# Second product of the last four tiles of the first block: from float32 to three float32r passes

## The chip, the cores and the metric

One core of one Trainium2 chip runs the kernel. The metric is the device time of one execution in microseconds (us); of several executions the median is taken. TensorE (PE) does the matrix products, VectorE (DVE) and ScalarE (ACT) the elementwise work, and SyncE (SP) issues the transfers.

## The reference

Two feed-forward layers follow a linear attention. Only the first layer's second product (`g @ w_out` of `_moe_ref`) is touched by the change.

```python
def _attn_ref(q, k, v, g_norm):
    kv = np.einsum('bhsd,bhse->bhde', k, v)
    out = np.einsum('bhsd,bhde->bhse', q, kv)
    rms = np.sqrt(np.mean(out * out, axis=-1, keepdims=True) + 1e-06)
    return (out / rms * g_norm).astype(np.float32)

def _moe_ref(x, w_in, w_out, a, b):        # 4608 tokens, 512 -> 2048 -> 512
    h = x @ w_in
    P = a[0] + a[1] * h + a[2] * h**2 + a[3] * h**3
    Q = 1.0 + np.abs(b[0]) * np.abs(h) + np.abs(b[1]) * h**2
    return ((P / (Q + 1e-06)) @ w_out).astype(np.float32)

def _moe2_ref(x, w_in, w_out):             # again 512 -> 2048 -> 512
    h = x @ w_in
    g = np.where(h >= 1, h, np.where(h <= -1, 0.0, (h + 1) ** 2 / 4))
    return (g @ w_out).astype(np.float32)
```

The attention's output, laid out as 4608 x 512, is the x of the first layer, whose output is the x of the second.

## The kernel before

**Stages.** Nine blocks of 512 tokens (`T`, `NB`) go through the first layer (phase 0, `ffn_step(0, j, f, s)`, block j), each in 16 tiles f of 128 hidden features (`NF`). After them block 0 goes through the second layer in the same manner (phase 1), and then the other eight blocks in pairs by a seven-product scheme (`ffn2_in`, `ffn2_out`), which uses combinations of weights and of activations that earlier stages prepare (`prepare`, `prepare_out`, `x_combinations`).

**A product in float32r.** A float32 value is split into a high part (a copy to float32r, made by ACT) and a low part (the difference, made by DVE). A product is then three matmuls: high by high, high by low, low by high. The first product of a tile is 4 such triples (lines 670 to 672) into the accumulator `h`, of which there are two (ring `h`): the first product of a tile cannot start before the tile two places earlier has been read out of its `h`, which DVE does last with the cubic's `t` (line 213, `t<-t,na,h`). The second product is 4 triples (lines 719 to 721) into `acc0` to `acc3`.

**The first block is different.** Its second products are made in float32 (`native`, line 717): 4 matmuls to a tile, which the chip runs as two records each, so 8 records to a tile. They need neither a split of `g` nor a split of the weights: DVE writes `gh` at once, and the decoded weight `w32[f]` (ring `wol`) is used as it is. The weights come packed and are decoded by `decode` (two ACT and two DVE instructions) while the first block runs. The high part of an output weight (ring `woh`) is made with the decoding; its low part by `weight_low`, with the key `NF + f + 0.5`, which places it one block later (line 312); the second block's second products need it.

**What sets the order.** Every instruction is recorded with a cost and a key. `Program.order` plays the list through: on each engine, whenever it comes free, the ready instruction with the lowest key is next. Tiles live in rings: the n-th tile of a ring of b buffers, counted by keys, waits for every reader of tile n - b. So a key or a count that changes in one ring can move instructions on all engines from there on.

**Rings that matter.** `wol` has 17 buffers (`NF + 1`): it holds five pieces of v at the very start, ten more of other batches, then the 16 decoded output weights and their 16 low parts, and later the 16 low parts of the second layer's output weights, which `prepare_out` makes (line 390) and also stores to DRAM for the last stage (`wod`). `dec` has 2 buffers, for weights being decoded. All transfers of these stages are issued by SP, in order.

Of the kernel before, what the change touches and what calls it, by code (L numbers as in the profile page):

```python
# [12 lines left out]
I32 = mybir.dt.int32  # L13
# [30 lines left out]
class Program:  # L44
# [16 lines left out]
    def op(self, engine, cost, key, fn, reads=(), writes=(), slack=0.0):  # L61
        i = len(self.ops)
        deps = set()
        for t in reads:
            if t.writer is not None:
                deps.add(t.writer)
            t.readers.append(i)
            getattr(t, "whole", t).ops.append(i)
        for t in writes:
            if t.writer is not None:  # L70
                deps.add(t.writer)
            deps.update(t.readers)
            t.writer, t.readers = i, []
            getattr(t, "whole", t).ops.append(i)
        deps.discard(i)
        self.ops.append((engine, cost, key, fn, deps, slack))
# [55 lines left out]
def kernel(  # L132
# [25 lines left out]
    NF = w1.shape[0]  # L158
# [2 lines left out]
    T = 512  # L161
    NB = NTOK // T
    LAG = 3
    NCH = (S + P - 1) // P
    EPS = 1e-6

# [18 lines left out]
    def new(ring, key, dtype=F32, shape=(P, T)):  # L185
        pool, bufs = (sb, RINGS[ring]) if ring in RINGS else (psum, PS_RINGS[ring])
        count[0] += 1
        name = f"{ring}_{count[0]}"
        return prog.buf(lambda: pool.tile(list(shape), dtype, tag=ring, name=name, bufs=bufs), ring, bufs, key)
# [62 lines left out]
    def load(key, t, src, cost=0.7, reads=(), rows=P):  # L252
        op(SP, cost, key, lambda: nc.sync.dma_start(out=t()[:rows], in_=src), reads, [t])
# [5 lines left out]
    def decode(key, raw, t, lb):  # L259
        def word(i):  # L260
            return raw().bitcast(I32).rearrange("p (n two) -> p n two", two=2)[:, :, i]

        def bias():
            nc.scalar.activation(out=t().bitcast(F32), in_=word(1).bitcast(F32), func=AF.Copy, scale=2.0**-112)

        def low_bits():
            nc.scalar.activation(
                out=lb().bitcast(I32), in_=raw().bitcast(U16).rearrange("p (n four) -> p n four", four=4)[:, :, 1], func=AF.Copy,
                scale=2.0**-13, bias=2.0**-14 - 0.5,
            )  # L270

        def shift_low():
            nc.vector.scalar_tensor_tensor(
                out=t(), in0=t(), scalar=3, in1=lb().bitcast(I32), op0=ALU.logical_shift_left, op1=ALU.bitwise_or
            )

        def sign():
            nc.vector.scalar_tensor_tensor(
                out=t(), in0=word(1), scalar=-0x80000000, in1=t(), op0=ALU.bitwise_and, op1=ALU.bitwise_or
            )  # L280

        op(ACT, 0.57, key, bias, [raw], [t])
        op(ACT, 0.57, key, low_bits, [raw], [lb])
        op(DVE, C_TT, key, shift_low, [lb], [t])
        op(DVE, C_TT, key, sign, [raw], [t])

    def weight(f, half, key):
        raw = new("raw", key, I64, (P, DM))

        t = new(("dec", "wol")[half], key, I32)  # L290
        hi = new(("wih", "woh")[half], key, F32R)
        load(key, raw, w1[f, half], 1.4)
        decode(key, raw, t, new("gl", key, I32))
        op(ACT, C_SB, key, lambda: nc.scalar.activation(out=hi(), in_=t().bitcast(F32), func=AF.Copy), [t], [hi])
        if half:
            w32[f] = t
            wsb[0, f, 1] = (hi, None)
        else:
            weight_low(f, half, key, t, hi)
# [3 lines left out]
    def weight_low(f, half, key, t, hi):  # L303
        if half:
            lo = new("wol", key, F32R)
        elif f < 4:
            if f % 2 == 0:
                wide[f // 2] = new("ow", key, F32R, (P, 2 * T))
            lo = Half(wide[f // 2], slice(f % 2 * T, (f % 2 + 1) * T))
        else:  # L310
            lo = new("wil", key, F32R)
        op(DVE, C_TT, key, lambda: nc.vector.tensor_tensor(
            out=lo(), in0=t().bitcast(F32), in1=hi().bitcast(F32), op=ALU.subtract
        ), [t, hi], [lo])
        wsb[0, f, half] = (hi, lo)
# [63 lines left out]
    def prepare_out(i, key):  # L379
# [45 lines left out]
        for n, (t, c) in enumerate(((s12, S1), (s34, S3))):  # L425
# [16 lines left out]
            for m in range(2):  # L442
# [5 lines left out]

    homes = {0: ("woh", "wol", 0), 2: ("woh", "wol", NCH), 4: ("woh", "wol", 2 * NCH),
             1: ("wih", "wil", 0), 3: ("wih", "wil", NCH)}  # L450

    def kv_batch(bb, key, step, gate=()):
        ps = new("m", key, shape=(P, NP, D))
        tiles = []
        for c in range(NCH):
            k0 = key + c * step
# [12 lines left out]
        def mm(some):  # L469
            for c, n, ts in some:  # L470
                kt, vt = (ts[0](), ts[1]()) if bb in homes else (ts[0]()[:, :DM], ts[0]()[:, DM:])
                for p in range(NP):
                    for o in range(0, P, D):
# [5 lines left out]
                            start=(c == 0 and p == 0),  # L479
                            stop=(c == NCH - 1),  # L480
                            skip_group_check=True,
                        )


        group = 1 if bb == 0 else NCH if bb in homes else 2
        for g0 in range(0, NCH, group):
            some = tiles[g0:g0 + group]
# [25 lines left out]
    def kv_fetch(bb, key):  # L513
        def fetch():

            for o in (0, D):
                for h in range(2):
                    nc.sync.dma_start(
                        out=kvbd[bb % 2]()[o:o + D, :, h * D:(h + 1) * D],
                        in_=kvd[bb, h * D:(h + 1) * D].rearrange("p (n d) -> p n d", d=D),  # L520
                    )

        op(SP, 2.0, key, fetch, [kvs[bb]], [kvbd[bb % 2]])
# [135 lines left out]
    def ffn_step(ph, j, f, s):  # L659
# [13 lines left out]

            op(PE, 0.68, s, in_mm, [whi, wlo, xh, xl], [h])
        k = s + 0.5
        native = ph == 0 and j == 0
        if ph == 0:

            ah, u, t, r = new("ah", k), new("u", k), new("t", k), new("r", k)
# [24 lines left out]
        if ph == 0 and j == 0:  # L704
            gs[f] = gh
        k = s + LAG + 0.5
        if f == 0:
# [3 lines left out]
        for m in range(4):  # L711
# [16 lines left out]
            if last:  # L728
                t = new("ow" if ph else "io", k)
# [237 lines left out]
    for f, half in order:  # L967
        weight(f, half, early.get((f, half), f - 2.8 + half * 2.7))
# [7 lines left out]
    for j in range(NB):  # L976
        s0 = j * NF
        if j == 1:
            kv_fetch(1, s0 - 1)
        if 2 <= j + 1 < B:  # L980
            kv_fetch(j + 1, s0 - 1)
        if j == 0:
            for p in range(KT):
                attention(1, p, 0.9 + 3.6 * p)
        elif j + 1 < NB:
            for p in range(0, KT, 2):
                attention_pair(j + 1, p, s0 + 2.5 + 3.8 * p, 3.8)
        for f in range(NF):
            ffn_step(0, j, f, s0 + f)

            if j == 0 and f % 2 == 1 and 3 + f // 2 < B:
                kv_batch(3 + f // 2, 3.05 + f, 0.45, [gs[f]])
            if j == 0:
                weight_low(f, 1, NF + f + 0.5, w32[f], wsb[0, f, 1][0])
        if j > 0:
            prepare(j - 1, s0 + 3)
# [8 lines left out]
    for f in range(NF):  # L1005
        ffn_step(1, 0, f, NS1 + f)
# [54 lines left out]
```

## Time and profile before

| | us |
|---|---|
| median of 3 runs | 1600.81 |
| lowest and highest | 1599.2, 1603.83 |
| the profiled execution | 1601.55 |
| its span, from the first to the last instruction | 1599.8 |
| PE busy | 1572.7 (98%) |
| DVE busy | 1437.7 (90%) |
| ACT busy | 1146.0 (72%) |

The profiled execution took 1.75 us more than its span, which lies around it, and 0.74 us more than the median. TensorE's granted clock was full throughout (0.999). A matmul's record is longer than the matmul holds the engine, since matmuls are pipelined; what one costs in a dense row of them is read from start to start. The same holds for DVE and ACT: a DVE record of 0.68 us is followed by the next start after 0.60 us.

Where the stages lie: phase 0's first block ends near 177 us, the ninth near 900 us, phase 1 runs to 972 us, and the last stage to the end.

### The profile page before, as it was taken

The page shows a single profiled execution, that of the slowest core. Times are in us where ns is not written, and L with a number is a line of the kernel's source. Part 1 is how long each engine was busy: PE and PEld are TensorE (multiplying, and loading weights), DVE is VectorE, ACT ScalarE, POOL GpSimd, SP SyncE. Part 2 cuts the span into 40 slices and gives each one's busy share as a digit, 9 for nine tenths or more (in the row PEclk, how much of TensorE's full clock was granted, in tenths as well). Part 3 has the DMA queues.
Part 4 walks back from the last instruction along what each step waited for, and adds up shares of the span by engine and source line. Part 5 has one row for each costly group of instructions (what it writes and reads, how often), then busy time and mean ns, then how long its engine had stood idle before and what let it go on. Part 6 is the DMA issues. An engine that isn't in the chain of part 4 may idle for free.

```text
span 1599.8 us, 22548 instructions
## 1 busy us (share of the span) xinstructions
PE 1572.7 (98%) x7504; PEld 1261.3 (79%) x7504; DVE 1437.7 (90%) x2330; ACT 1146.0 (72%) x1969; POOL 0.2 (0%) x4
## 2 busy tenths in 40 slices
PE   6999999999999999999999999999999999999998
PEld 3665788888888888888888887888888888888886
DVE  5999999999999999999999995799779977997787
ACT  6988888888888888888887874564457445645553
POOL 0000000000000000000000000000000000000000
PEclk9999999999999999999999999999999999999999
DMA  8967403021120302012064897677768776787674
GB/s 274 305 214 231 132 20 119 21 73 47 40 100 27 113 20 99 21 53 73 27 196 146 284 327 227 196 238 228 230 192 253 227 217 195 233 220 214 192 199 124
DMA packets 184180, 253.82 MB, mean 159 GB/s; under 512 B 56384, under 2 KB 95168, under 8 KB 184064
## 3 DMA queue, kind: packets, MB, share of 16 engines
q1 hardware_dynamic: 179840, 251.33, 50.6%
q10 hardware_dynamic: 4224, 1.05, 0.3%
q8 instruction: 60, 0.98, 0.2%
q14 instruction: 56, 0.46, 0.1%
HBM read 201.07 MB, written 51.25 MB: 158 GB/s over the span
## 4 chain that ended last, share of the span: by engine, by line
PE 81%; DVE 8%; DMA 4%; ACT 4%; issue 1%; SPq 1%; DVEq 0%; ACTq 0%
PE acc L807 17%; PE o L807 8%; PE h L670 7%; PE h L671 7%; PE h L672 7%; PE m L807 7%; PE h L807 6%; PE acc L719 6%; PE acc L720 6%; PE acc L721 6%; DMA raw<-in_w_dram 2%; DVE u L213 2%; PE acc L717 2%; DVE r L213 1%; DVE t L209 1%
## 5 line engine op out<-in xcount | busy, mean ns | idle before, releaser
L670 PE MATMUL h<-xh,wih 128*128 128x512 f32 x640 | 257.0, 402 | 4.1 <-DVE t L213 2.0
L671 PE MATMUL h<-xl,wih 128*128 128x512 f32 x640 | 249.3, 390 | 0.0
L719 PE MATMUL acc<-gh,woh 128*128 128x512 f32 x512 | 200.0, 391 | 0.0
L720 PE MATMUL acc<-gh,wol 128*128 128x512 f32 x512 | 199.3, 389 | 0.0
L721 PE MATMUL acc<-gl,woh 128*128 128x512 f32 x512 | 199.2, 389 | 0.0
L213 DVE SCALAR_TENSOR_TENSOR u<-u,r 128x512 f32<-128x512 f32 x272 | 185.7, 683 | 2.0 <-ACT r L199 1.0
L672 PE MATMUL h<-xh,wil 128*128 128x512 f32 x432 | 168.2, 389 | 0.0
L807 PE MATMUL acc<-raw,wih 128*128 128x512 f32 x720 | 166.2, 390 | 0.1
L807 PEld LDWEIGHTS acc<-raw,wih 128*128 128x128 f32 x720 | 134.9, 188 | 29.1 <-DVE raw L887 1.2
L670 PEld LDWEIGHTS h<-xh,wih 128*128 128x128 f32 x640 | 120.1, 188 | 37.1 <-DVE t L213 4.5
L671 PEld LDWEIGHTS h<-xl,wih 128*128 128x128 f32 x640 | 120.2, 188 | 27.1 <-issue 3.2
L199 ACT ACTIVATE r<-u 128x512 f32<-128x512 f32 x144 | 91.0, 632 | 63.3 <-DVE u L209 63.3
L885 ACT ACTIVATE raw<-dec 128x512 fp32r<-128x512 f32 x96 | 60.2, 633 | 80.9 <-DVE dec L883 49.0
L199 ACT ACTIVATE u<-ah,absb 128x512 f32<-128x512 f32 x144 | 117.8, 818 | 0.1
L719 PEld LDWEIGHTS acc<-gh,woh 128*128 128x128 f32 x512 | 96.1, 188 | 21.4 <-ACT ah L199 1.0
L199 ACT ACTIVATE t<-h,na 128x512 f32<-128x512 f32 x144 | 112.0, 778 | 0.0
L721 PEld LDWEIGHTS acc<-gl,woh 128*128 128x128 f32 x512 | 96.1, 188 | 20.0
L720 PEld LDWEIGHTS acc<-gh,wol 128*128 128x128 f32 x512 | 96.1, 188 | 19.7
L199 ACT ACTIVATE gh<-u 128x512 fp32r<-128x512 f32 x144 | 90.8, 631 | 24.3 <-DVE u L213 16.4
L213 DVE SCALAR_TENSOR_TENSOR r<-t,na,r 128x512 f32<-128x512 f32 x144 | 107.3, 745 | 0.9
L213 DVE SCALAR_TENSOR_TENSOR t<-t,na,h 128x512 f32<-128x512 f32 x144 | 106.4, 739 | 0.2
L204 DVE TENSOR_TENSOR gl<-u,gh 128x512 fp32r<-128x512 f32 x144 | 98.5, 684 | 4.8 <-ACT gh L199 2.9
(202 smaller groups left out, 3412.1 us busy)
## 6 DMA issues: line engine op xcount, KB each, us to landing
wih<-wd SPq DMA_DIRECT2D x256, 256.0 KB, 3.0
wih<-wod SPq DMA_DIRECT2D x224, 256.0 KB, 3.0
raw<-in_w_dram SPq DMA_DIRECT2D x64, 512.0 KB, 4.8
wd<-raw SPq DMA_DIRECT2D x48, 256.0 KB, 2.2
io<-x2d SPq DMA_DIRECT2D x44, 256.0 KB, 3.8
x2d<-io SPq DMA_DIRECT2D x36, 256.0 KB, 2.3
raw<-in_qT_dram SPq DMA_DIRECT2D x56, 128.0 KB, 3.0
out_dram<-ow SPq DMA_DIRECT2D x56, 128.0 KB, 3.4
```

The source lines that it names most:

```text
L199: op(ACT, cost, key, lambda: nc.scalar.activation(out=out(), in_=in_(), func=func, **{k: v() if callable(v) else v for k, v in kw.items()} ...
L204: op(DVE, C_TT, key, lambda: nc.vector.tensor_tensor(out=out(), in0=x(), in1=hi().bitcast(F32), op=ALU.subtract), [x, hi], [out])
L213: op(DVE, C_STT if callable(add) else C_TT, key, lambda: nc.vector.scalar_tensor_tensor(out=out(), in0=x(), scalar=add() if callable(add) ...
L670: nc.tensor.matmul(out=h(), lhsT=whi()[:, hc], rhs=xh(), start=(p == 0), stop=False)
L671: nc.tensor.matmul(out=h(), lhsT=whi()[:, hc], rhs=xl(), start=False, stop=False)
L672: nc.tensor.matmul(out=h(), lhsT=wlo()[:, lc], rhs=xh(), start=False, stop=(p == KT - 1))
L717: nc.tensor.matmul(out=o(), lhsT=wohi().bitcast(F32)[:, c], rhs=gh(), start=first, stop=last)
L719: nc.tensor.matmul(out=o(), lhsT=wohi()[:, c], rhs=gh(), start=first, stop=False)
L720: nc.tensor.matmul(out=o(), lhsT=wolo()[:, c], rhs=gh(), start=False, stop=False)
L721: nc.tensor.matmul(out=o(), lhsT=wohi()[:, c], rhs=gl(), start=False, stop=last)
L807: nc.tensor.matmul(out=bank(), lhsT=l, rhs=r(), start=(start and n == 0), stop=(stop and n == 2), skip_group_check=True,)
L885: op(ACT, C_SB, ke, lambda e=e, hi=hi: nc.scalar.activation(out=hi(), in_=e(), func=AF.Copy), [e], [hi])
```

## The change

`EXACT = NF - 4 = 12`. Only tiles 0 to 11 of the first block stay `native`. For tiles 12 to 15:

- the second product is 12 float32r matmuls in place of 4 float32 ones;
- `g` is split: DVE writes it to `u` instead of `gh`, ACT copies it to `gh`, DVE makes `gl`;
- the output weight is decoded into ring `dec` instead of `wol`, and its low part is made at once, with the decoding's key, instead of one block later.

```diff
+    EXACT = NF - 4
 ...
-        t = new(("dec", "wol")[half], key, I32)
+        keep = half and f < EXACT
+        t = new(("dec", "wol")[keep], key, I32)
 ...
-        if half:
+        if keep:
             w32[f] = t
             wsb[0, f, 1] = (hi, None)
         else:
 ...
-        native = ph == 0 and j == 0
+        native = ph == 0 and j == 0 and f < EXACT
 ...
-            if j == 0:
+            if j == 0 and f < EXACT:
                 weight_low(f, 1, NF + f + 0.5, w32[f], wsb[0, f, 1][0])
```

The number of low parts and of weight decodings stays the same. Ring `wol` gets four tiles fewer (the four decoded weights), and the four low parts come earlier in it. Line numbers of the change's rows are higher by one (lines 164 to 291) or by two (after 296): its line 721 is line 719 of before.

The order changes from the end of the first block on. Three places:

PE, at the end of the first block. `gh_1407` is tile 11, `h_1551` (`h_1562` in the change) the first product of tile 15. Before:

```order
L717 MATMUL acc_253_519<-gh_1407,wol_1299 128x512
L717 MATMUL acc_254_525<-gh_1407,wol_1299 128x512
L670 MATMUL h_1551<-xh_271,wih_1515 128x512
L671 MATMUL h_1551<-xl_280,wih_1515 128x512
L672 MATMUL h_1551<-xh_271,wil_1523 128x512
```

In the change:

```order
L719 MATMUL acc_257_519<-gh_1407,wol_1299 128x512
L719 MATMUL acc_258_525<-gh_1407,wol_1299 128x512
L721 MATMUL acc_255_503<-gh_1487,woh_1481 128x512
L722 MATMUL acc_255_503<-gh_1487,wol_1509 128x512
L723 MATMUL acc_255_503<-gl_1524,woh_1481 128x512
L672 MATMUL h_1562<-xh_271,wih_1519 128x512
```

Tile 12 (`gh_1487`) is now a product of three passes, and its first quarter stands ahead of tile 15's first product instead of behind it.

DVE, at the same time. `t_1480` (`t_1490`) is the cubic of tile 13, whose end frees the `h` that tile 15 needs. Before:

```order
L213 SCALAR_TENSOR_TENSOR gh_1510<-u_1365,r_1392 128x512
L204 TENSOR_TENSOR xl_1313<-a_243_1462,xh_1303 128x512
L312 TENSOR_TENSOR wil_1523<-dec_1466,wih_1515 128x512
L209 TENSOR_TENSOR u_1472<-u_1472,ah_1444 128x512
L209 TENSOR_TENSOR t_1480<-t_1480,h_1403 128x512
L273 SCALAR_TENSOR_TENSOR wol_1525<-wol_1525,gl_1531 128x512
L213 SCALAR_TENSOR_TENSOR t_1480<-t_1480,na,h_1403 128x512
```

In the change:

```order
L314 TENSOR_TENSOR wol_1509<-dec_1449,woh_1481 128x512
L279 SCALAR_TENSOR_TENSOR dec_1465<-raw_1425,dec_1465 128x512
L205 TENSOR_TENSOR xl_1313<-a_247_1461,xh_1303 128x512
L205 TENSOR_TENSOR gl_1524<-u_1365,gh_1487 128x512
L314 TENSOR_TENSOR wil_1529<-dec_1465,wih_1519 128x512
L210 TENSOR_TENSOR u_1472<-u_1472,ah_1443 128x512
L274 SCALAR_TENSOR_TENSOR dec_1526<-dec_1526,gl_1531 128x512
L210 TENSOR_TENSOR t_1490<-t_1490,h_1403 128x512
L279 SCALAR_TENSOR_TENSOR dec_1526<-raw_1479,dec_1526 128x512
L214 SCALAR_TENSOR_TENSOR t_1490<-t_1490,na,h_1403 128x512
```

The low parts of weight (`wol_1509`) and of `g` (`gl_1524`) of tile 12 have come in; the `t` that frees `h_1403` stands two rows later (row 208 of DVE's list instead of 206).

DVE, some 700 us later, in the ninth block: the low part that `prepare_out` makes of the second layer's output weight 1 (line 390; 392 in the change). Before, at the ninth block's eighth tile:

```order
L209 TENSOR_TENSOR t_8235<-t_8235,h_8201 128x512
L390 TENSOR_TENSOR wol_8271<-dec_7991,woh_8249 128x512
L204 TENSOR_TENSOR gl_8277<-u_8189,gh_8266 128x512
L213 SCALAR_TENSOR_TENSOR t_8235<-t_8235,na,h_8201 128x512
L213 SCALAR_TENSOR_TENSOR u_8241<-u_8241,r_8260 128x512
```

In the change, at the ninth block's sixteenth tile:

```order
L214 SCALAR_TENSOR_TENSOR t_8678<-t_8678,na,h_8648 128x512
L392 TENSOR_TENSOR wol_8706<-dec_8035,woh_8293 128x512
L205 TENSOR_TENSOR gl_8708<-u_8638,gh_8699 128x512
L214 SCALAR_TENSOR_TENSOR u_8684<-u_8684,r_8701 128x512
L274 SCALAR_TENSOR_TENSOR dec_8718<-dec_8718,kv_1722_8268 128x512
```

The low part of weight 1 has moved from row 1312 of DVE's list to row 1381 (counted with each list's own rows), since ring `wol` now gives it the buffer of tile 12's low part, which the ninth block reads nearly last. Low parts 2 to 5 move in the same way by fewer rows, and with all of them the stores to `wod` that read them; from weight 6 on the two lists run nearly level.

## Rows read from the trace of the kernel before

**Rows 1.** The page: busy time by engine, and busy tenths in 40 slices.

```profile
PE 1572.7 (98%) x7504; PEld 1261.3 (79%) x7504; DVE 1437.7 (90%) x2330; ACT 1146.0 (72%) x1969; POOL 0.2 (0%) x4
...
DVE  5999999999999999999999995799779977997787
```

**Rows 2.** Timeline of PE: start us, record us, instruction, [idle before <-releaser].

```profile
163.08 3.60 PE L717 MATMUL acc<-gh,wol 128*128 128x512 f32 x8
166.11 0.79 PE L670 MATMUL h<-xh,wih 128*128 128x512 f32 x1
166.74 0.40 PE L671 MATMUL h<-xl,wih 128*128 128x512 f32 x1
...
176.66 0.39 PE L719 MATMUL acc<-gh,woh 128*128 128x512 f32 x1
...
179.38 0.39 PE L670 MATMUL h<-xh,wih 128*128 128x512 f32 x1
179.60 0.39 PE L671 MATMUL h<-xl,wih 128*128 128x512 f32 x1
```

**Rows 3.** Weight loads of line 720: count, duration ns min/median/max.

```profile
L720 PEld LDWEIGHTS acc<-gh,wol x512: 187/188/189, 176.7 to 900.0; 128*128 128x128 f32 x171
```

**Rows 4.** Timeline of PE: the waits with a releaser from 140 us on.

```profile
145.76 0.47 PE L670 MATMUL h<-xh,wih 128*128 128x512 f32 x1 [0.49 <-DVE t L213]
...
191.35 0.50 PE L670 MATMUL h<-xh,wih 128*128 128x512 f32 x1 [0.48 <-DVE t L213]
...
906.17 0.50 PE L723 MATMUL acc<-woh,gh 128*128 128x512 f32 x1 [0.59 <-ACT io L199]
...
977.63 0.50 PE L807 MATMUL o<-xh,wih 128*128 128x512 f32 x1 [1.11 <-DVE a L814]
```

**Rows 5.** Windows: length, busy us (count) of PE, PEld, DVE, ACT, POOL, clock, DMA share, GB/s.

```profile
140.00:200.00 60.00, 59.03 (x288) 40.92 (x283) 58.64 (x98) 51.45 (x91) 0.00 (x0) 1.00 0.53 165
200.00:400.00 200.00, 199.90 (x950) 163.57 (x952) 195.33 (x317) 168.94 (x287) 0.00 (x0) 1.00 0.17 56
```

**Rows 6.** Timeline of DVE and of PE near the second block's tenth tile.

```profile
205.14 0.68 DVE L204 TENSOR_TENSOR gl<-u,gh 128x512 fp32r<-128x512 f32 x1
205.74 0.68 DVE L209 TENSOR_TENSOR t<-t,h 128x512 f32<-128x512 f32 x1
...
206.94 0.74 DVE L213 SCALAR_TENSOR_TENSOR t<-t,na,h 128x512 f32<-128x512 f32 x1
...
208.26 0.39 PE L670 MATMUL h<-xh,wih 128*128 128x512 f32 x1
```

**Rows 7.** Timeline of ACT: two copies to float32r that follow each other.

```profile
176.48 0.63 ACT L199 ACTIVATE a<-a 128x512 fp32r<-128x512 f32 x1
177.00 0.63 ACT L351 ACTIVATE raw<-dec 128x512 fp32r<-128x512 f32 x1
```

**Rows 8.** Windows at the end of phase 0 and in phase 1, columns as in rows 5.

```profile
900.00:971.00 71.00, 70.41 (x311) 57.97 (x310) 58.84 (x105) 51.54 (x92) 0.00 (x0) 1.00 1.00 336
900.00:930.00 30.00, 29.41 (x130) 24.02 (x129) 26.93 (x50) 24.11 (x45) 0.00 (x0) 1.00 1.02 359
```

**Rows 9.** The chain that ended last, near 900 us and where phase 1 ends: start, us, what.

```profile
900.34 5.08 DMA x2d<-io
...
971.04 0.69 DVE xl L204
971.75 3.77 DMA io<-x2d
975.54 0.69 DVE r L776
...
976.90 0.69 DVE a L814
```

**Rows 10.** Timeline of SP's queue: issues of transfers.

```profile
966.07 4.00 SPq L751 DMA_DIRECT2D wih<-wd  x6
971.15 1.26 SPq L253 DMA_DIRECT2D io<-x2d  x2
```

## The prediction

> **What bounds the kernel now.** I read the page's totals first, then the timeline of PE around the tiles that change, then who PE waited for, and last the windows of DVE and of the transfers. The totals show two engines near their limit: PE busy 98% of the span and DVE 90%, with DVE's slices full until about 1000 us [rows 1]. Which of them sets the time is read from start to start. In the stretch from 140 us on, matmuls follow each other without a hole but for a few named waits: two of some 0.5 us for DVE's `t` near 146 and 191 us, one of 0.59 us at 906 us for ACT's copy, which itself waits for a store, and one of 1.11 us at 977 us [rows 4]. So PE sets the time, and DVE is close behind: from 140 to 200 us it is busy 58.64 of 60 us, from 200 to 400 us 195.33 of 200 [rows 5]. A microsecond taken from PE is a microsecond won only as long as DVE, and further on the transfers, do not take its place.
>
> **The product itself.** The float32 product of tile 14 starts at 163.08, and the second matmul of what follows starts at 166.74: 3.66 us. The three-pass product that starts at 176.66 is followed by the second matmul of the next group at 179.60: 2.94 us [rows 2]. I take the second matmul of the next group since the first one's record is stretched after a float32 product (0.79 us against 0.39). The difference is 0.72 us to a tile; four tiles give **-2.9 us** (2.88) on PE, and this is the whole of what the change can save by itself.
>
> A rule speaks against it, and the rows decide. The twelve weight loads of a three-pass product last 0.188 us each [rows 3], and yet its matmuls follow each other every 2.72 us / 12 = 0.227 us (176.66 to 179.38, [rows 2]); so the loads lie beside the matmuls. The Trainium skill, "TensorE: Matmul & The Clock Gate", section "The mechanism" of its Part 3, says that a weight load overlaps running matmuls only where the row group differs, which it does not here. By that rule a three-pass tile would take 12 x (0.227 + 0.188) = 4.98 us and the float32 tile with its 8 loads 3.66 - 0.227 + 8 x 0.188 = 4.94 us, and the change would save nothing; this case's trace disagrees with it, by 2.72 us against 4.98.
>
> **What DVE and ACT get.** For each of the four tiles one DVE subtract (`gl`) and one ACT copy (`gh`) are new. A DVE instruction costs 0.60 us from start to start (205.14 to 205.74, [rows 6]), an ACT copy 0.52 (176.48 to 177.00, [rows 7]): 4 x 0.60 = 2.4 us of DVE, 4 x 0.52 = 2.1 us of ACT. ACT is busy 51.45 us of 60 there [rows 5], 8.5 us are free, and I cost its copies at nothing; if ACT had no room, they would cost 2.1 us at most. Making the weights' low parts earlier adds no instruction; it moves four of 0.60 us forward, and the order pushes other low parts back.
>
> DVE has 60 - 58.64 = 1.36 us free from 140 to 200 us [rows 5], so it cannot take 2.4 us there unnoticed, unless other work is put off. What counts is the `t` that frees `h`. The tightest place that I find in the two orders is the second block's eighth tile: its `t` ends at 206.94 + 0.74 = 207.68, and the tile that needs that `h` starts at 208.26, 0.58 us later [rows 6]. In the new order one DVE row more stands ahead of that `t` (0.6 us), and PE has 1.8 us less ahead of that start: 0.58 - 0.6 - 1.8 = -1.8 us. The 1.36 us of free time of DVE can fill up before a matmul waits, so a new wait of 0.4 to 1.8 us; the present waits of 0.49 and 0.48 at 146 and 191 us may also go, since other work now stands in front of both, which is the lower end, -1.0. I take **+0.8**, since part of the 1.36 us is DVE waiting for ACT and cannot be filled. After 200 us DVE has 4.67 us free in 200 us [rows 5], so that the loss does not grow.
>
> **What moves 700 us later.** Ring `wol` has four tiles fewer ahead of the second layer's low parts. Low part 1 now gets the buffer of tile 12's low part, which the ninth block reads nearly last. No product waits for this: by the order low part 1 is made at the ninth block's sixteenth tile and needed some five tiles later, and the last ones are made as early as before within a tile. What moves with them are transfers. Up to the first store of the ninth block's output (near 900 us) the new order of SP has ten stores of 128 KB and one load of 512 KB fewer, and up to the twelfth read of `x2d` the two lists are level again. So 1.84 MB more go into the stretch from 900 to 971 us, in which the transfer engines are already busy all the time (share 1.00, 336 GB/s, 23.9 MB) [rows 8]. At 336 GB/s the 25.7 MB need 76.5 us, 5.5 us too many; at the 359 GB/s of the first 30 us [rows 8] they need 71.6, 0.6 us too many.
>
> Who waits for that: the two reads of `x2d` at 971 us are last in the chain into the last stage, 3.77 us of landing, then DVE, then PE's wait of 1.11 us [rows 4, 9]. Ahead of them SP has some room: six issues from 966.07 end at 970.07, and the reads are issued at 971.15, after DVE has freed their buffer [rows 9, 10]; 1.1 us at least. So the term lies between -1.1 (the present wait goes, if the queue is shorter) and 5.5 - 1.1 = +4.4. I take **+1.0**: nearer to the low rate's remainder than to the high one, and about the size of the wait that stands there. The wait at 906 us stays: the same transfers stand just before that store.
>
> **Sum.** -2.9 + 0.8 + 1.0 = -1.1 us. The profiled execution took 1601.55 (span 1599.8 and 1.75 around it), so 1600.5 on its own scale; it was 0.74 above the median, so against the median 1600.81 - 1.1 = **1599.7 us**, 0.07% less. About 0.3% (4.8 us) is what a measurement of this kernel can tell from no change, and the runs of before themselves lie between 1599.2 and 1603.83. My forecast is therefore no difference that can be told.
>
> **The rivals.**
>
> *DVE takes PE's place in the first two blocks.* If none of the eight DVE instructions that are new or moved forward hides, 8 x 0.60 = 4.8 us stand against 2.9: +1.9, and with the 1.0 of the end +2.9, 1603.7 us. For it: 58.64 of 60 us. Against it: DVE idles 4.67 us in the next 200 [rows 5], and the order puts other low parts off.
>
> *The transfers hold up the last stage.* Slower: the full 5.5 us arrive at the reads of 971 us, and their landing grows from 3.77 to the 5.08 us of the store at 900 us [rows 9], another 1.3 us: -2.9 + 0.8 + 5.5 + 1.3 = +4.7, 1605.5 us. It decides where SP has not reached the twelfth read of `x2d` when DVE frees its buffer. For it: share 1.00 over 71 us [rows 8]. Against it: 128 KB stores that SP issues one by one are spread wider in the new order, and the first 30 us of the stretch show 359 GB/s.
>
> *The new order also removes the old waits.* All four of rows 4 go, 0.49 + 0.48 + 0.59 + 1.11 = 2.7 us, and nothing comes in their place: -2.9 - 2.7 = -5.6, 1595.2 us. For it: a product now stands ahead of the first of them. Against it: three of the four hang on buffers that the change does not free earlier.
>
> *Nothing is saved.* The weight loads do not hide in these four tiles, or PE waits for `gl` just as long as it saves: 0 with the small terms, 1601 to 1603 us. The three-pass tiles of the next block, dense at 2.72 us [rows 2], speak against the first form, which is the skill's rule above; I give that form 0.01.
>
> **How the numbers follow.** Forecast 0.60; DVE in front 0.10; transfers 0.13; old waits removed 0.09; nothing saved 0.08 (0.01 of it the rule's form). Faster by over 0.3% (below 1596.0) takes most of the old-waits case and a tail of the forecast: 0.08. Slower by over 0.3% (above 1605.6) takes half of the transfers' case and a tail of DVE's: 0.10. The rest, 0.82, is within 0.3%. Range: at the low end both open terms at their lower bounds give -2.9 - 1.0 - 1.1 = -5.0, 1595.8; at the high end 1.8 and 4.4 give +3.3, 1604.1, and I go to 1604.5 for the scatter of the median. Outside lie the far parts of the two outer cases.
>
> **What the changed kernel's profile would show.** Right: the last four tiles of the first block in 12 records each, 2.72 us apart from the next group; the second block's first three-pass product some 2 us earlier than at 176.66 [rows 2]; at 200 to 400 us PE without holes; near 975 us a wait of 1 to 3 us. Wrong: new waits of `h` for `t` of more than 2 us in all between 140 and 260 us (DVE's case), a wait of 4 us or more at the start of the last stage with reads of `x2d` that are issued late (the transfers' case), or holes of PE in phase 1 for low parts of the second layer's weights, which I cost at nothing.

## The result, and the profile after

The changed kernel takes 1611.88 us (median of 6, 1610.54 to 1613.55) against 1600.49 us (median of 6) for the kernel before: ratio 1.0059, 95% interval 1.0046 to 1.0071. The medians are 11.4 us apart; the ratio, which is not the quotient of the two medians, stands for some 9.5 us. The forecast was 1599.7 and its range ended at 1604.5. The profiled execution took 1611.24 us with a span of 1609.4, 9.6 us more than the 1599.8 of before.

The totals say nothing of it. From the page, the busy time of each engine and the slices of DVE, to be held against [rows 1]:

```profile
PE 1571.7 (98%) x7520; PEld 1265.9 (79%) x7520; DVE 1441.3 (90%) x2334; ACT 1146.8 (71%) x1973; POOL 0.2 (0%) x4
...
DVE  5999999999999999999999895799789977997787
```

PE is even busy 1 us less than before, in a span that is 9.6 us longer. The loss is therefore in the time in which PE waits. The view of waits of PE from 130 to 1000 us (who waits for whom, us in total, times, longest) shows them:

```profile
PE o L809 <- DVE a L816: 6.5, 1, 6.5
PE h L672 <- DVE t L214: 4.5, 3, 2.6
PE acc L725 <- ACT io L200: 1.6, 1, 1.6
```

They are the three kinds of [rows 4], and each has grown: 1.11 to 6.5 us at the start of the last stage, 1.0 to 4.5 us for `t`, 0.59 to 1.6 us for the copy near 907 us. The windows (columns as in [rows 5]) show the same places, and one thing more, in the third column from the end:

```profile
140.00:200.00 60.00, 55.96 (x300) 43.87 (x296) 55.71 (x92) 49.97 (x89) 0.00 (x0) 0.97 0.34 108
200.00:400.00 200.00, 199.53 (x944) 162.79 (x943) 196.93 (x324) 169.14 (x291) 0.00 (x0) 1.00 0.23 73
...
980.00:1000.00 20.00, 13.49 (x54) 10.95 (x54) 10.03 (x16) 6.07 (x10) 0.00 (x0) 0.83 0.52 167
```

The granted clock is below 1.00 in exactly the two windows with the long waits (before: 1.00 in both).

To place the loss I compared the start of the same matmul in two traces. At 139 us the changed kernel is 0.46 us behind, and at 142 us, ahead of its first changed matmul (144.81), 0.11 us. What it makes good in between is nothing of the change: in the trace of before one product, `m<-raw`, takes 0.36 us longer than here (the PE timelines of before and after):

```profile
138.74 1.51 PE L475 MATMUL m<-raw 128*64 128x64 f32 x32
```

```profile
139.20 1.15 PE L477 MATMUL m<-raw 128*64 128x64 f32 x32
```

At the matmul that before starts at 880.03 (in the ninth block of phase 0) it is 2.57 us behind (882.60), and this number stands still from 345 to 900 us. At the matmul of before's 995 us it is 10.41 us behind. So **2.5 us are lost between 142 and 345 us**, where 2.1 were to be won, **and 7.8 us from 900 to 990 us**. Of the 2.5 us, 1.1 come only in the third block, between 330 and 345 us, where PE waits once more for a `t` (0.47 us at 342.81). Some 0.7 us come back between 1000 us and the end, as they do in most of the kernels below; I did not follow them up.

**The first two blocks.** Timeline of PE in after: a three-pass tile of the first block, and then the wait:

```profile
157.20 0.39 PE L721 MATMUL acc<-gh,woh 128*128 128x512 f32 x1
...
159.69 0.39 PE L723 MATMUL acc<-gl,woh 128*128 128x512 f32 x1
...
163.74 0.79 PE L672 MATMUL h<-xh,wih 128*128 128x512 f32 x1 [2.63 <-DVE t L214]
164.33 0.63 PE L673 MATMUL h<-xl,wih 128*128 128x512 f32 x1
164.76 0.63 PE L674 MATMUL h<-xh,ow 128*128 128x512 f32 x1
...
167.45 0.40 PE L672 MATMUL h<-xh,wih 128*128 128x512 f32 x1
167.69 0.39 PE L673 MATMUL h<-xl,wih 128*128 128x512 f32 x1
```

The tile is as dense as was said: 11 steps from matmul to matmul between 157.20 and 159.69, 0.227 us each. Then PE waits 2.63 us for DVE's `t`, and after that its matmuls follow each other every 0.427 us (164.33 to 164.76) until 167, where it is 0.23 again: the granted clock is at half, 1.2 GHz in place of 2.4, for about 3.5 us, which costs 1.6 us more. Who held `t` up is in the timeline of ACT:

```profile
156.95 0.82 ACT L200 ACTIVATE u<-ah,absb 128x512 f32<-128x512 f32 x1
160.29 0.69 ACT L265 ACTIVATE dec<-raw 128x512 f32<-128x512 f32 x1 [2.52 <-DVE t L210]
160.89 0.61 ACT L200 ACTIVATE gh<-u 128x512 fp32r<-128x512 f32 x1
161.53 0.78 ACT L200 ACTIVATE t<-h,na 128x512 f32<-128x512 f32 x1
```

ACT stands idle for 2.52 us in front of `dec<-raw`, the first step of a decode for `prepare`, which nobody needs soon. The view names DVE's `t` of 159.55 as the releaser; but the load of this `raw` was issued at 154.58 and landed at 160.21 (5.63 us), 0.08 us before the decode starts. `gh` and ACT's `t` of the gate stand behind it in ACT's row, DVE's `t` (162.34) waits for ACT's, and PE for DVE's.

**The start of the last stage.** The chain that ended last, there (start, us, what):

```profile
979.27 0.03 issue
979.30 5.15 DMA io<-x2d
...
984.54 0.70 DVE r L778
...
985.88 0.69 DVE a L816
...
986.61 2.93 PE o L809 x6
```

It is the chain of [rows 9] with two differences. The read of `x2d` is issued at 979.30 in place of 971.15: of these 8.15 us 3.58 are the lag that the program had by then, 4.57 are new. And it takes 5.15 us to land in place of 4.36. (The 3.77 us in [rows 9] are not a landing time: that row starts at 971.75, and the read that DVE waits for was issued at 971.15 and landed at 975.51.) The two add up to 5.4 us. Ahead of the read SP issues without a pause from 961.84 us on (timeline of SP's queue):

```profile
964.79 0.64 SPq L403 DMA_DIRECT2D wod<-woh  x1
965.48 0.78 SPq L403 DMA_DIRECT2D wod<-wol  x1
...
975.58 0.46 SPq L403 DMA_DIRECT2D wod<-woh  x1
976.08 0.45 SPq L403 DMA_DIRECT2D wod<-wol  x1
...
977.84 0.42 SPq L254 DMA_DIRECT2D io<-x2d  x1
...
979.30 0.86 SPq L254 DMA_DIRECT2D io<-x2d  x2
```

In [rows 10] the six issues ahead of the reads are loads of `wd`, and SP is idle for a microsecond before the reads; here the last stores of the second layer's weights stand just ahead of them. The sum: 5.4 us of wait (6.51 - 1.11), 1.0 near 907 us (1.6 - 0.59), and 1.4 of half clock behind the wait: from the first start of the stage's matmuls to the eighth it is 3.13 us (986.61 to 989.74) and was 1.73 before (977.63 to 979.36). 5.4 + 1.0 + 1.4 = 7.8.

Why the stores come late is in DVE's timeline. The second low part of the late preparation (line 390 of before, line 392 of after), before and after:

```profile
843.13 0.68 DVE L390 TENSOR_TENSOR wol<-dec,woh 128x512 fp32r<-128x512 f32 x1
```

```profile
887.65 0.69 DVE L392 TENSOR_TENSOR wol<-dec,woh 128x512 fp32r<-128x512 f32 x1
```

It is 44 us later, and the last but one, made at 950.20 before, is made at 961.89. The ring of 17 `wol` buffers is handed out in the order of the keys, and a buffer is had when its holder of 17 places before is through. With four entries fewer, this low part follows the early low part of tile 12, which the last block reads nearly last; before, it followed that of tile 0.

### The profile page after: what moved, and what is told of

Same layout as the page of the kernel before. It is cut to its first block, busy times and chain, and to the rows that moved or that the text cites. A ratio compares the mean times of both kernels' runs of the same rounds, so it can differ in the third digit from the quotient of the medians.

```text
span 1609.4 us, 22558 instructions
## 1 busy us (share of the span) xinstructions
PE 1571.7 (98%) x7520; PEld 1265.9 (79%) x7520; DVE 1441.3 (90%) x2334; ACT 1146.8 (71%) x1973; POOL 0.2 (0%) x4
## 4 chain that ended last, share of the span: by engine, by line
PE 92%; DMA 3%; DVE 2%; ACT 2%; issue 0%; SPq 0%; DVEq 0%; ACTq 0%
PE acc L809 17%; PE h L672 9%; PE h L673 8%; PE h L674 8%; PE o L809 8%; PE acc L721 7%; PE acc L722 7%; PE acc L723 7%; PE m L809 7%; PE h L809 6%; PE acc L719 2%; DMA raw<-in_w_dram 1%; PE m L477 1%; PE acc L725 1%; PE acc L727 1%; PE acc L726 1%
## 5 line engine op out<-in xcount | busy, mean ns | idle before, releaser
L721 PE MATMUL acc<-gh,woh 128*128 128x512 f32 x528 | 206.7, 392 | 0.0
L722 PE MATMUL acc<-gh,wol 128*128 128x512 f32 x528 | 205.5, 389 | 0.0
L723 PE MATMUL acc<-gl,woh 128*128 128x512 f32 x528 | 205.4, 389 | 0.0
```

The source lines that it names most:

```text
L721: nc.tensor.matmul(out=o(), lhsT=wohi()[:, c], rhs=gh(), start=first, stop=False)
L722: nc.tensor.matmul(out=o(), lhsT=wolo()[:, c], rhs=gh(), start=False, stop=False)
L723: nc.tensor.matmul(out=o(), lhsT=wohi()[:, c], rhs=gl(), start=False, stop=last)
```

## The experiments

A table of all of them first. "At 142", "at 880" and "at 995" is how far the matmul that before starts at 142, 880.03 and 995 us starts later in that kernel's trace than in before's; what is there at 142 us is there ahead of the first changed product. The ratio is that of the times to the kernel before on the same chip; it is not the quotient of the two medians. Each trace is one execution.

| kernel | at 142 | at 880 | at 995 | 900 to 995 | median us | ratio, 95% interval |
|---|---|---|---|---|---|---|
| changed kernel | 0.11 | 2.57 | 10.41 | 7.8 | 1611.88 | 1.0059 (1.0046 to 1.0071) |
| the same again | 0.29 | 2.96 | 11.10 | 8.1 | 1612.01 | 1.0067 (1.0054 to 1.0079) |
| old ring places | 0.10 | -0.71 | -0.71 | 0.0 | 1600.30 | 0.9982 (0.9972 to 0.9992) |
| before, new ring places alone | -0.61 | 13.38 | 21.84 | 8.5 | 1623.98 | 1.0141 (1.0121 to 1.0161) |
| decode with slack | -0.16 | -0.92 | 6.99 | 7.9 | 1609.76 | 1.0042 (1.0029 to 1.0055) |
| merged stores | -0.34 | -0.78 | 2.58 | 3.4 | 1607.70 | 1.0029 (1.0016 to 1.0042) |
| old places and slack | 0.64 | 1.68 | 0.80 | -0.9 | 1600.32 | 0.9997 (0.9985 to 1.0008) |
| old places and merged stores | -0.41 | -0.67 | -0.92 | -0.3 | 1599.66 | 0.9987 (0.9976 to 0.9998) |
| old places, eight tiles | 1.82 (at 100) | 11.64 | 11.81 | 0.2 | 1613.19 | 1.0075 (1.0062 to 1.0089) |
| old places, two tiles | -0.15 | -1.33 | -1.96 | -0.6 | 1600.60 | 0.9996 (0.9985 to 1.0007) |
| new places, two tiles | 0.61 | -0.17 | 8.89 | 9.1 | 1607.91 | 1.0041 (1.0027 to 1.0054) |

### Is it the place in the ring?

The changed kernel with one line altered:

```diff
-            lo = new("wol", key, F32R)
+            lo = new("wol", max(key, NF + f + 0.5), F32R)
```

> The changed kernel, with one number altered: the low output weights of tiles 12 to 15, which it now decodes in the first block, keep the place in the ring of `wol` buffers that they had before (the key that assigns a buffer is again that of the late decode). The three passes, their early decode and everything of the first block stay; the late weight preparation asks for the same buffers at the same time as in the kernel before, so its loads and stores stand on SP in the old order from the third block on. Theory 1 (the wait of 6.67 us at the start of the last stage comes from the late preparation having been moved forward by the freed buffers, so that SP is still issuing its stores when the reads of `x2d` are due): the wait falls back from 6.67 to about 1.3 us, the stretch at half clock behind it (about 1.4 us) and 1.0 us of the wait near 905 us go with it, in sum 7.8 us: about 1604 us against 1611.9 of the changed kernel and 1600.5 of the one before (ratio 1.002). The wait of 2.63 us at 160.84 us stays. Theory 2 (the late wait is a result of the first block, whose lateness shifts the whole row of transfers): no change, about 1612 us (1.007).

It is the place. From 900 us on this kernel loses nothing against before, its second low part is made at 842.4, and at the end PE's waits (130 to 1000 us) are the old ones; those of `h` for `t` are 2.0 us, where they were 1.0 before and 4.5 in the changed kernel:

```profile
PE h L672 <- DVE t L214: 2.0, 3, 1.0
PE o L809 <- DVE a L816: 1.2, 1, 1.2
PE acc L725 <- ACT io L200: 0.5, 1, 0.5
```

(The expectation's 6.67 us is the wait of 6.51, counted from where the next matmul of a dense row would have started.) At ratio 0.9982 the interval lies below 1, as it does with merged stores on top (0.9987): the three passes pay, but by less than the 0.3% that the prediction took as the least that can be told, and two further kernels with the old places, with the slack and with two tiles, can't be told from before. It gained more than expected, since the wait at 160.84 us is gone too, which was not to go (in its order one of ACT's `t` stands ahead of the decode and not behind it, and the load lands at 158.16). And the expectation tells the direction wrong: the freed buffers move the preparation back, not forward, as the rows on the low part show.

The opposite half, the kernel before with nothing but the new places:

```diff
-            lo = new("wol", key, F32R)
+            lo = new("wol", key if f < NF - 4 else NF + 0.01 * f, F32R)
```

> The kernel before with only the other half of the change: all products stay in float32 and the low output weights of tiles 12 to 15 are still made late, but their key in the ring of `wol` buffers is the early one of the changed kernel, so the late weight preparation gets its buffers as early as there. SP's order from the third block on is then that of the changed kernel, and the first block that of the kernel before. Theory 1 (freed buffers move the preparation's stores in front of the reads of `x2d`): the start of the last stage waits some 6 us where it waited 1.27, with a stretch at half clock behind it: plus 6 to 8 us, about 1607 to 1608 us, ratio 1.004 to 1.005. Theory 2 (the late wait follows from the first block): 1600.5 us, ratio 1.000.

From 900 us on it loses 8.5 us, a little more than the 6 to 8 of theory 1 (PE's waits from 400 us on):

```profile
PE o L807 <- DVE a L814: 5.2, 1, 5.2
PE acc L723 <- ACT io L199: 2.1, 1, 2.1
```

But it also loses some 14 us in the first blocks, which I had not expected and which is this experiment's own: the twelve other low parts all move four places back in the ring, and wait for float32 products of the first block (PE's waits from 130 to 400 us):

```profile
PE o L543 <- ACT a L199: 4.6, 1, 4.6
PE acc L720 <- DVE wol L312: 3.6, 2, 2.9
```

The 3.6 us are for low parts themselves; that the 4.6 us for ACT's `a` follow from them was not shown. Behind the two longest of these waits PE's clock is at half, from 190.3 to 193.7 and up to 214.2 us. So its total says nothing of the change, its stretch from 900 us on does.

### What is short ahead of the reads: SP's issues or bytes?

```diff
-                for h in range(n + 1):
-                    for o, x in ((0, hi), (HW, lo)):
-                        nc.sync.dma_start(out=wod[i, cs[h], :, o:o + HW], in_=x().bitcast(F32)[:, h * HW:(h + 1) * HW])
+                for o, x in ((0, hi), (HW, lo)):
+                    if n == 0:
+                        nc.sync.dma_start(out=wod[i, cs[0], :, o:o + HW], in_=x().bitcast(F32)[:, 0:HW])
+                    else:
+                        nc.sync.dma_start(
+                            out=wod[i, cs[0]:cs[1] + 1:2, :, o:o + HW].rearrange("c p n -> p c n"),
+                            in_=x().bitcast(F32).rearrange("p (c n) -> p c n", n=HW),
+                        )
```

> The changed kernel, with the stores of the late weight preparation merged: for every second weight the four stores of 128 KB become two of 256 KB, the same bytes to the same places, 16 issues fewer on SP, and no other instruction or order altered. It asks what SP is short of ahead of the reads of `x2d`. Theory 1 (SP's own time for each issue: from 961 to 982 us it issues back to back, about 0.45 us for a store of 128 KB, while landing times fall to 2.1 to 2.7 us): with 2 issues fewer for each pair the reads are issued 1 to 4 us earlier and the wait of 6.67 us shrinks by as much, 1608 to 1611 us, ratio 1.005 to 1.006. Theory 2 (the bytes: the 16 transfer engines are busy 95% and more, and an issue on SP is only as slow as the queues are full): the two stores take as long as the four did, no change, about 1612 us, 1.007.

SP's issues. A store of 256 KB takes SP about as long as one of 128 KB, and the reads go out earlier (SP's queue in this kernel), 1.2 us late against its own lag where they were 4.57 late:

```profile
960.84 0.44 SPq L405 DMA_DIRECT2D wod<-woh  x1
961.32 0.51 SPq L405 DMA_DIRECT2D wod<-wol  x1
...
971.85 0.86 SPq L254 DMA_DIRECT2D io<-x2d  x2
```

Of the 7.8 us 4.5 are gone, with the same bytes: the wait at the last stage is 2.6 us in place of 6.5, which is within the 1 to 4 us of theory 1, and the rest is at the copy near 905 us (0.8 in place of 1.6). The half clock behind the shorter wait costs no less (1.6 us; 1.4 in the changed kernel); 980 to 1000 us is granted 0.92 here and 0.83 there, where the clock fell while PE still waited. The low parts are as late as in the changed kernel (the second at 884.31), so it is not they that came earlier. The ratio of 1.0029 is lower than theory 1 had it (1.005 to 1.006), since the loss of the first blocks is missing from this trace too (-0.78 at 880.03); the traced execution, 1604.88 us, is one of the faster of twelve. With the old ring places the same merging finds nothing to win in the whole time:

> The kernel with the old ring places and with the merged stores (16 issues fewer on SP, same bytes). It asks whether SP's issues also set what is left of the wait at the start of the last stage, 1.41 us with the old ring places alone, where six loads stand on SP right before the reads. Theory 1 (SP's issues set that wait too): it shrinks by up to 1 us, 1599.3 us. Theory 2 (the reads wait for their buffer, which VectorE frees, not for SP): 1600.3 us, no change. Merging was worth 4.5 us of the trace where the stores stood late; if it is worth nothing here, the late stores and not SP's work as such were the cause.

1599.66 against 1600.30 without it, with intervals that overlap almost wholly (0.9976 to 0.9998, 0.9972 to 0.9992). On the wait itself theory 1 is right: in its trace the wait at the last stage is 0.2 us (1.2 without the merging). But the wait near 905 us is 0.8 (0.5 without), and PE loses another 0.45 us between 920 and 960 us, so that of the 1 us only 0.2 is left at 995 us. So SP's issues cost 4.5 us here where late stores stand ahead of the reads, and at most 1 us where none do.

### The decode in ACT's row

```diff
-            decode(key + 1 + n, raws[n], ts[n], ss[n])
+            decode(key + 1 + n, raws[n], ts[n], ss[n], 4.0)
...
-        op(ACT, 0.57, key, bias, [raw], [t])
+        op(ACT, 0.57, key, bias, [raw], [t], slack=slack)
```

> The changed kernel, with a slack of 4 us given to the planner for the first ScalarE operation of each decode in the preparation of the next block's input weights, so that it puts this operation behind the gate work of the first block and not ahead of it while its load is still on the way. Nothing is computed otherwise. Theory 1 (the PE wait of 2.63 us at 160.84 us is ScalarE standing at that decode for a load that lands at 160.21 us, with `gh` and `t` of the gate queued behind it; the half clock from 163.7 to 167 us comes after it): wait and half clock go, about minus 3.5 us, 1608.4 us, ratio to the kernel before 1.005. The wait at the start of the last stage stays near 6.7 us. Theory 2 (VectorE has too much work there, the decode only happens to stand first): the wait only moves by some tenths of a microsecond or turns up a row later at the same size, 1611 to 1612 us, 1.007.

Ratio 1.0042 against 1.0059 (the intervals overlap), and 3.5 us less at 880.03 us of the trace (2.57 to -0.92), the size that was expected; the loss from 900 us on stays (7.9), as expected. That would settle it, but two other kernels lost the same wait without any slack, the one with merged stores with the decode just where it was (-0.78 at 880.03), and in all three of these traces the load lands early, at 158.1 to 158.5 us. So this trace does not show what the slack is worth, and the changed kernel ran once more:

> The changed kernel once more, unaltered. Two other kernels with the same first block (the one with the old ring places and the one with merged stores) ran their profiled execution without the wait of 2.63 us at 160.84 us: there the load of `raw` landed 4.5 and 4.1 us after its issue, at 158.2 and 158.1 us, and in the changed kernel 5.63 us after it, at 160.21. Theory 1 (the wait is a matter of the single execution, of how long that load takes): in this profiled execution the wait is below 1 us where the load lands before 159 us, and the runs lie between 1608 us (without the 3.5 us of wait and half clock) and 1612 us. Theory 2 (it belongs to the order): wait near 2.6 us again and all runs at 1610.5 to 1613.6 us. The loss of about 7.8 us from 900 to 990 us is there in either case.

Theory 2 has the numbers: the wait is there again, somewhat shorter, with the half clock behind it, and all eleven runs of the changed kernel lie between 1610.5 and 1613.6. In both its profiles the load lands at the same late time (160.21 and 160.11 us; issued 154.58 and 154.12).

```profile
163.63 0.50 PE L672 MATMUL h<-xh,wih 128*128 128x512 f32 x1 [2.03 <-DVE t L214]
```

But ACT's idle time is not in the same place. In this second profile it stands 2.13 us in front of the decode of the block's own last tile, whose load landed at 157.08 (155.27 the first time), and only 0.65 us in front of the decode for `prepare`:

```profile
157.10 0.66 ACT L265 ACTIVATE dec<-raw 128x512 f32<-128x512 f32 x1 [2.13 <-DMA raw<-in_w_dram]
...
160.19 0.68 ACT L265 ACTIVATE dec<-raw 128x512 f32<-128x512 f32 x1 [0.65 <-DMA raw<-in_w_dram]
```

In the kernel with merged stores, whose instructions stand in the same order until long after, the same load was issued at 153.91 and landed at 158.05, and ACT waits 0.86 us, not 2.52:

```profile
156.47 0.80 ACT L200 ACTIVATE u<-ah,absb 128x512 f32<-128x512 f32 x1
158.13 0.67 ACT L265 ACTIVATE dec<-raw 128x512 f32<-128x512 f32 x1 [0.86 <-DMA raw<-in_w_dram]
```

So what is shown is this: the order puts two decodes ahead of the gate's work, and what that costs hangs on when their loads land, for the second one 158.1 or 160.2 us, for issues that are only 0.2 to 0.7 us apart. Why the load lands by 2 us later in the one case is open. The runs of the merged kernel spread from 1603.0 to 1611.7, so it may show both cases; no trace tells that.

Both repairs together:

> The changed kernel with the old places in the ring for the four early low parts, and the slack of 4 us for the decode of the next block's input weights: both repairs at once. Theory 1 (the two losses are separate, and the decode's loss appears in some executions only): nothing is left to win against the repair of the ring alone but those executions, 1599 to 1600.3 us, ratio 0.998. Theory 2 (moving the decode puts other work of the first block late): a new wait between 160 and 300 us, 1601 to 1603 us.

Between the two: no faster than the old places alone (0.9997 against 0.9982, with intervals that overlap). Its trace has a wait of 0.85 us at 455.01 for ACT's `a`; the traces without the slack do not have it, but neither does that of the slack alone, so that it is the slack's was not shown.

### What a tile is worth, and what number of tiles means for the end

Both are the kernel with the old places, with `EXACT = NF - 8` and `EXACT = NF - 2`.

> The kernel with the old ring places, and eight tiles of the first block in three passes where it had four. It asks what a tile is worth. Theory 1 (PE alone counts): another 4 x 0.72 = 2.9 us go, 1597.4 us against 1600.3 for four tiles, ratio 0.9965. Theory 2 (VectorE takes PE's place: it is busy 59.44 of 60 us from 140 to 200 us with four tiles, and each tile brings one more subtract of 0.60 us and moves another one forward): the gain is eaten by waits of `h` for VectorE's `t`, up to 4 x 1.2 = 4.8 us: 1600 to 1602 us, ratio 0.998 to 1.000.

Slower than before by 0.75%: far beyond both theories. PE now waits for things of the tiles themselves, and not only for `h` (130 to 400 us):

```profile
PE m L477 <- DVE a L214: 2.4, 1, 2.4
PE acc L722 <- DVE wol L314: 1.2, 1, 1.2
PE acc L721 <- ACT gh L200: 1.1, 1, 1.1
PE acc L723 <- DVE gl L205: 1.0, 1, 1.0
```

and from 140 to 200 us the granted clock is 0.94. Ahead of these stands a wait of 1.84 us at 126.51 for ACT's `wih`, with half clock from 128.2 to 131.6 us. Of the 11.6 us, 1.8 are there at 100 us already, where PE's order is still that of before; they were not followed up. From 900 us on it loses 0.2 us: with the old places the number of tiles does not matter there.

> The kernel with the old ring places, and two tiles of the first block in three passes where it had four (eight made it 12 us slower than before, with VectorE's low parts and gate work late in the first block). Theory 1 (a tile saves 0.72 us on PE, and the two waits of `h` for `t`, 1.18 and 0.83 us with four tiles, come only with VectorE's added work and shrink with it): minus 1.4 us at 400 us of the trace and about the same time as four tiles, 1599.7 to 1600.8 us, ratio 0.998 to 1.000. Theory 2 (with four tiles VectorE is already over its limit): two tiles beat four by 1 us or more, 1598 to 1599 us, ratio 0.997.

As theory 1 has it. From -0.15 at 142 us to -1.33 at 880.03 it gains 1.2 us with two tiles, near to 2 x 0.72 = 1.44 (two waits of some 0.5 us have gone and two have come). Four tiles with the same places gain 0.8 (0.10 to -0.71). So the first two tiles pay most of their price, and the third and fourth pay nothing: there the two waits of `h` come in (1.01 us at 147.77 and 0.67 at 282.35, which the expectation counts as 1.18 and 0.83 from where a dense row would have gone on). Half a microsecond is also what two traces of one first block differ by: with merged stores on top the same four tiles gain 0.3. In the measured time the two kernels can't be told apart (0.9985 to 1.0007, 0.9972 to 0.9992).

The last one is the changed kernel with `EXACT = NF - 2` and its own, new places:

> The changed kernel with two tiles in place of four, and the ring places as the change leaves them (new ones). It asks whether the loss at the end of the second layer goes with the number of tiles or with the place. In the traces so far the new places make the second low part of the late preparation wait for the buffer of a tile that the last block reads nearly last: it is made at 887.7 us where it was made at 843.1, and the last ones at 961.9 and 964.0 where they were made at 950.2 and 953.3. (An earlier expectation told this the wrong way round, as a move forward; it is a move back.) With two tiles the second low part takes tile 14's buffer, later still, and the rest follows just as late. Theory 1 (place): the loss between 900 and 990 us is as with four tiles or larger, 7 to 10 us, against about minus 1 us won before: 1607 to 1611 us, ratio 1.004 to 1.006. Theory 2 (number of tiles): half the loss, about 4 us: 1603 to 1604 us, 1.002.

Theory 1: 9.1 us from 900 to 995 us with half the tiles. The second low part is made at 894.4 us, the last ones at 965.8 and 967.9, and the wait is 7.0 us (PE's waits from 400 us on):

```profile
PE m L809 <- DVE a L816: 7.0, 1, 7.0
```

## Why the prediction was wrong, step by step

**The product, -2.9 us: right.** 0.227 us from matmul to matmul in the changed tiles, and 1.2 us net for two tiles, against 1.44. The weight loads hide, as the rows said, and the rule of the Trainium skill that was set against them ("TensorE: Matmul & The Clock Gate", section "The mechanism") is not borne out here. The same section also names the background weight buffer, into which a load may go ahead of running matmuls; the prediction left that case out, and the rows don't speak against it.

**DVE and ACT in the first two blocks, +0.8: too small, in two steps.** The waits for `t` that DVE's added work brings are real, and in the kernel with the old places (-0.8 us in all, against -2.9) the term is +2.1, above its upper bound of 1.8. Half of it comes where the prediction said that the loss does not grow, after 200 us: PE loses 1.0 us between 280 and 300 us there, and the changed kernel 1.1 between 330 and 345 us. What was missed besides is the sentence "I cost its copies at nothing": it asked whether ACT had time, 8.5 us in 60, and not what stood in front of what. ACT stood 2.52 us at a decode whose load had not landed, with the gate's work behind it in its row. That and the half clock are what the traces show for the other 3.3 us: the term measured +5.3 in the changed kernel (2.46 + 2.88). How much of it the order of ACT's row costs by itself stays open, since loads landed early in the trace that was to tell.

**What moves 700 us later, +1.0: the failing step, 7.8 us measured.** The mechanism was found: ring `wol`, low part 1 behind tile 12's, ten stores moved to behind 900 us, the reads of `x2d` held up, and the rival on it names the place and the sign. What failed is the price. It was worked out from bytes (1.84 MB at 336 or 359 GB/s), and the room from SP's pause of 1.1 us as if SP only had to wait for the engines. SP is what was short: the ten stores at some 0.5 us from start to start (975.58 to 976.08 and the like) and a load are about 5 us of SP's own time, against 1.1 us of room, and the reads went out 4.57 us late. The merged stores show it, same bytes and 4.5 us less; 3.4 us stay with them. To the 4.57 come 0.8 us of longer landing (the transfers' rival had 1.3, worked out from the row of 3.77 us, where 4.36 is the landing time), 1.4 us of half clock, which nobody had, and 1.0 us near 907 us, where the text said that the wait stays.

**The chances.** The two rivals that were slower were priced as exclusive, +2.9 and +4.7; here both came at once and each larger than its price, 5.3 us against 4.8 in the first blocks (3.3 of them with ACT's decode and the half clock, which that rival did not have) and 7.8 against 6.8 at the end. The prediction said that a wait of 1 to 3 us at the last stage would show it right, and a wait of 4 us or more with late reads, or new waits of `h` for `t` of over 2 us between 140 and 260 us, would show it wrong. The trace has both signs of being wrong: 6.51 us with late reads, and 1.41 + 2.63 us of `h` where 0.97 were.

## What to carry to other kernels

A change that makes something earlier also frees or takes a place in a ring, and the next user of that place may be hundreds of microseconds away: print who follows whom in the ring before and after, and keep the old place if the new one follows a buffer that is read late. Price transfers that move ahead of a read twice, by bytes and by issues on the queue, and take the larger one. Room on an engine is no cover: look at which instruction stands ahead of the one that counts, and whether its load can be late.

## What the runs showed of the hardware

- After long waits of PE the granted clock was at half, 1.2 GHz, and matmuls that follow each other every 0.227 us took 0.427. It was so after the waits of 2.03 and 2.63 us near 161 us, of 1.84 us at 126.51 with eight tiles, and of 2.57, 5.22, 6.51 and 7.01 us at the last stage; in the changed kernel from about 164 to 167 us and up to 989.7, at 1.6 and 1.4 us on top of the wait, and after the wait of 5.22 us up to 1002.7, for 6 us. It was not after the waits of 1.1 and 1.2 us at the last stage, nor after those of 1.7 us near 147.5 in three kernels, nor after one of 2.12 us that ended at 921.08 in the kernel with the new ring places alone. So a wait's price can be more than its length, and the length alone does not tell when.
- The stores of 256 KB in the merged kernel took SP 0.47 us to issue in the median (14 from 900 to 982 us, 0.42 to 0.96), those of 128 KB in the changed kernel 0.43 (40, 0.32 to 1.11): a store of twice the size took SP hardly longer.
- The same load, issued 0.2 to 0.7 us later in the changed kernel than in the one with merged stores, landed 2 us later (160.1 to 160.2 us against 158.05); this was not explained.
